# Sliding-window attention with a token-mixing MLP: q in one load per batch, queries reordered inside blocks, transposes on halves of the array, merged products, relus and copies, a new hand-written order

## The chip, the core and the metric

The kernel runs on one core of one Trainium2 chip. The metric is device time in microseconds of one execution, lower is better. A profile is one execution recorded by the hardware; its span runs from the first to the last instruction of the core.

The engines that matter: PE (TensorE; its weight loads are shown as PEld), DVE (VectorE), ACT (ScalarE), POOL (GpSimd, which here issues casting loads), and SP (SyncE, which issues stores).

## The reference, cut to what matters

q, k and v are 8 batches x 8 heads x 576 tokens x 64. Attention sees the last 128 tokens, with a linear distance bias per head; the heads' outputs are laid side by side as x (576 x 512 per batch), and x is mixed over tokens.

```python
scores = q @ k^T / 8                                     # per batch and head
scores = where(0 <= i - j < 128, scores - slope_h * |i - j|, -1e9)
attn   = softmax(scores)
x      = (attn @ v) with heads side by side              # (8, 576, 512)
wq, wk = x @ moe_w_q, x @ moe_w_k                        # (8, 576, 64)
mixed  = (wq @ wk^T / 8) @ x                             # = wq @ (wk^T @ x) / 8
out    = relu(mixed) @ moe_w_out                         # (8, 576, 512), f32
```

## The kernel before

Everything on chip is f16 except PSUM and the output. A batch's tokens are cut into four blocks of 128 and a tail of 64; tails of two batches (a pair, `pr`) are handled together, and so is the MLP of a pair. One operation (`Op`) is a short list of instructions for one engine; the whole sequence of operations is written out by hand in `ORDER`, one word per operation: its name, its batch and part, then the engine (P, A, D, G or S) and, for TensorE, which of the 4 PSUM pairs (of 2 banks each) or which single bank it writes. Each engine runs its operations in the order of that text, and semaphores join engines where data or banks are shared. So a change of `ORDER` moves every engine's queue.

The operations, by name:

- Loads. `LF`: the first tiles of batch 0 in f32 through SP and ACT. `Lq`, `Lk`, `Lv`, `Lt` (tails of q and k of a pair, two transfers): on GpSimd, with a cast to f16 on the way. Each moves 128 tokens of 8 heads, as 1024 pieces of 64 elements. `Lw`, `Lwo`: the MLP's weights in f32 through SP into output buffers (`osb`), cast by DVE in `CWQ` and `CW`.
- `TQ` (L474, transposes of q and k of one block by a product with the identity, 8 of 128x128, into one bank), copied out by `ETQ`; `TF`, `TJ` the same for batch 0, `TT`/`ETT` for tails, on the lower 64 rows of the array.
- `QK` (unit of key block g, four heads u): scores transposed, keys on partitions. Two heads share the array: one on rows 0 to 63, one on rows 64 to 127, writing two banks. `EXP` (L587) on ACT evicts 1024 columns; `MUL` (L594) on DVE multiplies them by a table `bias` of exp(-slope distance), zero outside the window (`biasl` for the last key blocks).
- `PV`: context of a block of queries; the 65th column of v is 1, so the sum of the weights comes along. `RC` takes the reciprocal, `X` (L634) evicts x. For the 64 tail queries all eight heads go into 64 partitions.
- `XT`/`EXT` and `XTT`/`EXTT`: transposes of x and their copies. `WQ`, `WK`, `WT`: projections of x, of a pair, and of its tails. `G`: wk^T x. `MX`: G with wq into mixed, transposed; two batches use the two row halves. `RM`, `RMT` (L770, L772): relu, 512 columns each. `OUT`: by moe_w_out, four products of 512 columns; `EO` evicts it into `osb`, `DO` stores it through SP.
- `WM`: products on zeros that keep TensorE busy at the start.

`wk`'s tail is kept with zeros in the other batch's rows (`pads`), since both tails lie in one tile. `NNAT` = 4, `NV` = 4 and `NPT` = 5 say how many buffers q and k tiles, v tiles and score tiles have; `OSB` = 12 output buffers.

The parts that decide the mode in which the array is used are the slices of the operands:

```python
mm(ps[:, e, ...], t[64 * e:64 * e + 64, 1, hp, ...], t[64 * e:64 * e + 64, 0, hp, ...])   # QK: row halves
mm(pw[64 * e:64 * e + 64, :], wqk_sb[:, c, 0:64], xT_s[b % NX][:, c, :])                  # WQ: column halves
tp(dst[:, j, c, :], src[j][:, 2 * c:2 * c + 2, :], identh)                                # TQ: whole array
```

Of the kernel before, what the change touches and what calls it, by code (L numbers as in the profile page):

```python
# [25 lines left out]
NNAT = 4  # L26
NV = 4
NPT = 5
PTW = 1088
# [4 lines left out]
OSB = 12  # L34
WIDE = ()

WARM = (12, 3, 4, 3, 3, 5,)

ORDER = """
warm:D LF0.0.1.0:A ident:G LF0.0.1.1:A LF0.1.0.1:S ones:D LF0.1.0.0:S Lk0.1:G LF0.0.0.1:S  # L40
LF0.0.0.0:S Lq0.2:G pads:D zeros:D Lt0:G WM.0:P31 TF0.1.1:P00 idh:D TF0.1.0:P01 iota:G Lk0.2:G
wmc:D WM.1:P31 TF0.0.1:P10 EF0.1.0:D EF0.1.1:D mask:G TF0.0.0:P01 EF0.0.1:A Lq0.3:G bias:A
EF0.0.0:D Lk0.3:G WM.2:P31 TJ0.2.0:P00 TJ0.1.1:P01 EJ0.2.0:D QK0.0.1:P1 Lq1.1:G EJ0.1.1:D
QK0.1.1:P0 QK0.0.0:P2 Lv0.0:G EXP0.1.1:A biasl:D TT0:P30 Lq1.2:G TJ0.2.1:P31 EXP0.0.0:A
QK0.1.0:P0 Lk1.1:G EJ0.2.1:D EXP0.0.1:A ETT0:D TJ0.3.0:P31 Lk1.2:G EXP0.1.0:A EJ0.3.0:D ETT1:D
WM.3:P21 TJ0.3.1:P10 Lv0.1:G QK0.2.1:P2 EJ0.3.1:D QK0.2.0:P3 MUL0.1.0:D QK0.3.1:P1 EXP0.2.0:A
Lk1.0:G QK0.3.0:P0 MUL0.0.0:D Lq1.0:G EXP0.2.1:A MUL0.2.0:D MUL0.0.1:D Lk1.3:G EXP0.3.1:A
MUL0.2.1:D PV0.0:P2 Lq1.3:G TQ1.1:P30 EXP0.3.0:A RC0.0:D MUL0.1.1:D TQ1.2:P31 Lv0.2:G ETQ1.1:D
ETQ1.2:A MUL0.3.1:D PV0.1:P0 Lv0.3:G X0.0:D QK1.1.0:P3 Lk2.1:G QK1.1.1:P1 RC0.1:D MUL0.3.0:D
EXP1.1.0:A TQ1.0:P20 Lq2.1:G X0.1:D EXP1.1.1:A ETQ1.0:D XT0.0:P21 Lv1.0:G QK1.0.0:P0 EXT0.0:D  # L50
Lq2.2:G TQ1.3:P20 EXP1.0.0:A MUL1.1.1:D QK1.0.1:P1 PV0.2:P3 Lk2.2:G ETQ1.3:D EXP1.0.1:A
MUL1.0.0:D QK1.2.1:P2 Lv1.1:G QK1.3.1:P0 RC0.2:D EXP1.2.1:A PV0.3:P1 X0.2:D Lq2.3:G RC0.3:D
QK1.2.0:P3 X0.3:D QK1.3.0:P2 Lk2.3:G EXP1.3.0:A MUL1.0.1:D TQ2.1:P10 Lv1.2:G MUL1.1.0:D
EXP1.3.1:A PV1.0:P2 MUL1.2.1:D XT0.1:P11 Lv1.3:G RC1.0:D MUL1.3.0:D EXT0.1:A Lv0.4:G TQ2.2:P00
ETQ2.1:D Lq2.0:G ETQ2.2:A X1.0:D WM.4:P01 PV1.1:P1 MUL1.3.1:D Lv1.4:G EXP1.2.0:A QK2.1.0:P0
QK2.1.1:P2 wz:D RC1.1:D Lw:S Lk2.0:G X1.1:D EXP2.1.0:A TQ2.3:P30 MUL1.2.0:D Lk3.1:G Lwo.1:S
XT1.0:P31 EXP2.1.1:A Lwo.3:S ETQ2.3:D PV1.2:P0 Lt1:G Lwo.2:S PV1.3:P1 EXT1.0:A RC1.2:D Lwo.0:S
X1.2:D PV0.4:P2 RC1.3:D RC0.4:D QK2.2.0:P0 X1.3:D Lq3.1:G EXP2.2.0:A X0.4:D Lk3.0:G WM.5:P30
PV1.4:P1 XT1.1:P31 RC1.4:D X1.4:D QK2.2.1:P0 Lq3.0:G EXT1.1:A XTT0:P30 CWQ:D Lv2.0:G TQ2.0:P10
EXP2.2.1:A EXTT0:D WK0:P31 ETQ2.0:D Lq3.2:G MUL2.1.1:D QK2.0.1:P1 EWK0:A Lk3.2:G QK2.0.0:P0  # L60
MUL2.2.0:D WT0:P30 EXP2.0.1:A WQ0:P31 Lv2.1:G EWT0:D EXP2.0.0:A MUL2.0.1:D G0:P30 CW.1:D EWQ0:A
CW.2:D TT2:P00 MUL2.0.0:D EG0:A Lv2.4:G ETT2:D MX0.4:P3 MX0.1:P1 ETT3:D MX0.0:P2 RMT0:A RM0.1:D
MX0.2:P0 RM1.0:A Lk3.3:G MX0.3:P3 RM0.2:D TQ3.1:P10 RM0.0:A RM0.3:D RM1.2:A Lq3.3:G QK2.3.1:P2
RM1.1:A CW.0:D QK2.3.0:P0 CW.3:D TQ3.0:P30 EXP2.3.1:A Lv2.2:G ETQ3.1:D OUT0.3:P11 ETQ3.0:D
Lk4.2:G EXP2.3.0:A PV2.0:P2 MUL2.1.0:D OUT0.1:P10 Lv3.1:G RM1.3:A RC2.0:D MUL2.3.0:D EO0.3:A
QK3.0.0:P3 Lv2.3:G QK3.0.1:P0 X2.0:D EXP3.0.0:A OUT1.0:P11 MUL2.3.1:D Lv3.0:G EO0.1:A TQ3.2:P20
MUL3.0.0:D OUT0.2:P21 EXP3.0.1:A Lk4.1:G ETQ3.2:D PV2.1:P3 Lq4.2:G EO1.0:A MUL3.0.1:D EO0.2:A
QK3.1.0:P0 QK3.1.1:P1 RC2.1:D Lq4.1:G MUL2.2.1:D EXP3.1.0:A TQ3.3:P20 X2.1:D OUT0.0:P21 Lv3.2:G
EXP3.1.1:A ETQ3.3:D PV2.2:P3 Lq4.0:G MUL3.1.0:D EO0.0:A QK3.2.1:P0 QK3.2.0:P1 RC2.2:D
EXP3.2.1:A Lq4.3:G OUT1.3:P21 X2.2:D MUL3.1.1:D Lv3.3:G EXP3.2.0:A PV2.3:P3 MUL3.2.1:D PV3.0:P0  # L70
OUT1.4:P20 Lk4.3:G EO1.3:A RC2.3:D RC3.0:D X2.3:D Lk4.0:G QK3.3.1:P1 X3.0:D EO1.4:A QK3.3.0:P3
XT2.0:P21 EXP3.3.0:A MUL3.2.0:D Lv3.4:G PV3.1:P0 EXT2.0:D TQ4.2:P20 Lt2:G EXP3.3.1:A MUL3.3.0:D
TQ4.1:P30 XT2.1:P21 RC3.1:D ETQ4.2:A MUL3.3.1:D OUT1.1:P31 Lv4.1:G ETQ4.1:D PV3.2:P1 EXT2.1:D
EO1.1:A Lk5.0:G OUT1.2:P30 RC3.2:D X3.1:D Lv4.0:G PV3.3:P2 X3.2:D EO1.2:A QK4.1.1:P0 Lv4.2:G
RC3.3:D TQ4.3:P30 X3.3:D EXP4.1.1:A QK4.1.0:P1 Lk5.1:G ETQ4.3:D PV2.4:P2 EXP4.1.0:A XT3.0:P31
RC2.4:D TQ4.0:P30 Lq5.0:G X2.4:D EXT3.0:A PV3.4:P0 ETQ4.0:D QK4.2.0:P2 Lq5.1:G XT3.1:P10
RC3.4:D EXP4.2.0:A X3.4:D QK4.2.1:P3 Lq5.3:G TT4:P11 EXT3.1:D EXP4.2.1:A QK4.0.1:P0 Lk5.3:G
XTT2:P20 MUL4.1.1:D WK2:P10 EXP4.0.1:A EXTT2:D Lk5.2:G ETT5:D WT2:P20 ETT4:D EWK2:A Lq5.2:G
MUL4.2.0:D QK4.0.0:P0 QK4.3.1:P3 EWT2:A QK4.3.0:P1 MUL4.2.1:D EXP4.0.0:A WQ2:P21 Lq6.3:G
MUL4.1.0:D EXP4.3.1:A G2:P20 Lv4.3:G MUL4.0.1:D MUL4.0.0:D EWQ2:A Lk6.0:G PV4.2:P3 MUL4.3.1:D  # L80
# [77 lines left out]
def kernel(  # L158
# [53 lines left out]
    def natv(b, j, n):  # L212
        return nat_s[(b // 2) % 2][j][n][:, b % 2]
# [13 lines left out]
    def hold(i):  # L227
        held.append(i.ins)
# [686 lines left out]
```

## Time and profile before

| | us |
|---|---|
| three runs: median (lowest, highest) | 141.13 (140.97, 143.18) |
| the profiled execution | 141.15 |
| its span | 139.3 |
| TensorE clock granted, mean over the span | 0.987 |
| mean of one MUL (128x1024) on DVE, 64 of them | 0.68, 0.67 |
| mean of one EXP (128x1024) on ACT, 64 of them | 1.03 |
| mean of one RM (128x512) on ACT, 25 of them; on DVE, 7 | 0.65; 0.68 |
| mean of one output eviction on ACT, 35 of them; on DVE, 1 | 0.60; 0.69 |
| mean of one x eviction, 128x512, 32 of them; of the tails, 64x512, 8 | 0.69; 0.69 |
| transfers of q, k, v, tails on GpSimd | 30, 31, 40, 8 |
| landing of a q tile, a k tile, a v tile, half a pair's tails (medians) | 5.1, 5.3, 5.5, 7 to 8 |

How to read it: matmuls are pipelined and their ends are modelled, so a duration of a matmul holds some 0.2 us in which the next has begun; from start to start they are much shorter. On DVE and ACT neighbours overlap by about 0.1. The slices are 40 equal parts of the span, each digit the busy share in tenths.

### The profile page before, as it was taken

To read this page: it belongs to the slowest core of one execution; us is meant where nothing else is said; L and a number is where in the kernel's file an instruction comes from. 1 tells how busy PE (TensorE), PEld (TensorE's weight loads), DVE (VectorE), ACT (ScalarE), POOL (GpSimd) and SP (SyncE) were. 2 spreads that over 40 slices of the span, in tenths; PEclk is the share of its full clock that TensorE was granted. 3 is DMA by queue.
4 is the path that set the end of the run, shared out by engine and by line. 5 is a ranking of instruction groups with operands and counts; after the bars stand their busy time and mean duration, and the time that the engine had idled before them with its cause. 6 is when DMAs were issued, how large, how long until landed. Compare 5 with 4: busy or idle time off the path is not lost.

```text
span 139.3 us, 4479 instructions
## 1 busy us (share of the span) xinstructions
PE 125.9 (90%) x1846; PEld 84.5 (61%) x1846; DVE 114.1 (82%) x254; ACT 112.2 (81%) x165; POOL 95.6 (69%) x118
## 2 busy tenths in 40 slices
PE   6778599879987999999999999999999999999970
PEld 4445486768744566767866477667765656754420
DVE  5657999999996999999999999999998999705000
ACT  3089969898796999868999999978989995279860
POOL 7999999999919999999999999759940000000000
PEclk9999869999999999999999999999999999999999
DMA  4999999999999999999999999999999975505993
GB/s 103 184 155 154 157 153 153 152 150 177 283 184 156 152 155 152 151 153 150 152 151 154 147 172 270 232 202 152 157 171 272 338 274 216 226 5 171 335 355 121
DMA packets 119332, 25.59 MB, mean 184 GB/s; under 512 B 114192, under 2 KB 114192, under 8 KB 119312
## 3 DMA queue, kind: packets, MB, share of 16 engines
q0 software_dynamic: 109264, 13.77, 155.9%
q1 hardware_dynamic: 8992, 11.28, 24.2%
q10 hardware_dynamic: 1056, 0.26, 0.8%
q8 instruction: 14, 0.23, 0.6%
q14 instruction: 6, 0.05, 0.1%
HBM read 29.62 MB, written 9.44 MB: 280 GB/s over the span
## 4 chain that ended last, share of the span: by engine, by line
PE 58%; POOL 22%; DMA 7%; DVE 7%; issue 2%; ACT 1%; ACTq 0%; POOLq 0%
PE pair L231 47%; POOL nat L363 13%; PE pair L234 11%; DMA natt<-in_k_dram 7%; POOL vt L380 6%; DVE pt L594 3%; DVE qkT L240 2%; POOL natt L370 2%; ACT osb L238 1%; DVE x L634 1%; DVE xT L240 0%; DVE rm L772 0%; POOL wm L298 0%; DVE xTt L240 0%; POOL wm L300 0%
## 5 line engine op out<-in xcount | busy, mean ns | idle before, releaser
L587 ACT ACTIVATE pt<-pair 128x1024 f16<-128x1024 f32 x64 | 62.8, 1033 | 4.0 <-PE pair L231 3.6
L380 POOL DMA_DIRECT2D vt<-in_v_dram x40 | 36.9, 976 | 2.6 <-PE pair L231 2.4
L363 POOL DMA_DIRECT2D nat<-in_k_dram x31 | 30.8, 1036 | 3.5 <-DMA nat<-in_k_dram 3.4
L231 PE MATMUL pair<-wout_sb,rm 128*128 128x512 f16 x128 | 31.6, 379 | 0.0
L594 DVE TENSOR_TENSOR pt<-pt,bias 128x1024 f16<-128x1024 f16 x48 | 31.3, 680 | 0.1
L363 POOL DMA_DIRECT2D nat<-in_q_dram x30 | 30.4, 1039 | 0.3 <-DMA vt<-in_v_dram 0.3
L238 ACT COPY osb<-pair 128x512 f32<-128x512 f32 x35 | 20.7, 601 | 7.4 <-PE pair L231 7.2
L231 PEld LDWEIGHTS <-pt 128*128 128x128 f16 x576 | 21.4, 98 | 8.4 <-issue 2.7
L231 PE MATMUL pair<-vt,pt 128*128 128x65 f16 x576 | 24.1, 195 | 2.3 <-ACT pt L587 1.6
L240 DVE COPY qkT<-pair 128x1024 f16<-128x1024 f16 (+1 forms) x38 | 21.7, 591 | 2.6 <-PE pair L231 1.3
L231 PE MATMUL pair<-qkT 64*128 64x256 f16 (+2 forms) x320 | 21.5, 250 | 1.1 <-DVE x L634 0.5
L634 DVE TENSOR_TENSOR x<-pair,inv 128x512 f16<-128x512 f32 x32 | 21.6, 685 | 0.5
L234 PE MATMUL pair<-identh,nat 128*128 128x128 f16 x244 | 19.3, 226 | 1.4 <-ACT pt L587 0.7
L234 PEld LDWEIGHTS <-nat 128*128 128x128 f16 x244 | 15.2, 101 | 5.8 <-issue 3.6
L231 PEld LDWEIGHTS <-rm 128*128 128x128 f16 x128 | 11.1, 97 | 10.6 <-issue 0.8
L231 PEld LDWEIGHTS <-qkT 64*128 64x128 f16 x320 | 11.3, 94 | 7.7 <-issue 3.2
L770 ACT ACTIVATE rm<-pair 128x512 f16<-128x512 f32 x25 | 13.7, 647 | 0.0
L594 DVE TENSOR_TENSOR pt<-pt,biasl 128x1024 f16<-128x1024 f16 x16 | 10.7, 668 | 0.0
L234 PE MATMUL pair<-identh,x 128*128 128x128 f16 x128 | 9.9, 219 | 0.0
L648 DVE RECIPROCAL inv<-pair 128x8 f32<-128x8 f32 (+1 forms) x40 | 7.8, 200 | 1.2 <-PE pair L231 0.8
L234 PEld LDWEIGHTS <-x 128*128 128x128 f16 x128 | 7.6, 98 | 1.7 <-issue 0.8
L240 DVE COPY xT<-pair 128x1024 f16<-128x1024 f16 x12 | 8.2, 687 | 0.4 <-PE pair L234 0.2
(66 smaller groups left out, 116.7 us busy)
## 6 DMA issues: line engine op xcount, KB each, us to landing
out_dram<-osb SPq DMA_DIRECT2D x32, 256.0 KB, 3.0
vt<-in_v_dram POOLq DMA_DIRECT2D x32, 128.0 KB, 5.5
nat<-in_k_dram POOLq DMA_DIRECT2D x31, 128.0 KB, 5.3
nat<-in_q_dram POOLq DMA_DIRECT2D x30, 128.0 KB, 5.1
osb<-in_moe_w_out_dram SPq DMA_DIRECT2D x4, 256.0 KB, 7.2
out_dram<-osb SPq DMA_DIRECT2D x8, 128.0 KB, 3.9
osb<-in_q_dram SPq DMA_DIRECT2D x4, 128.0 KB, 3.8
natt<-in_q_dram POOLq DMA_DIRECT2D x4, 128.0 KB, 7.1
```

The lines of the kernel that those rows point to most:

```text
L231: hold(nc.tensor.matmul(*a, **k))
L234: hold(nc.tensor.transpose(*a))
L238: hold(nc.scalar.copy(out_ap, in_ap))
L240: hold(nc.vector.tensor_copy(out=out_ap, in_=in_ap))
L363: return lambda: nc.gpsimd.dma_start(out=natv(b, j, n), in_=(q, k)[j][b, :, P * n:P * n + P, :].transpose([1, 0, 2]))
L370: nc.gpsimd.dma_start(out=natt_s[pr % 2][:, j].rearrange("p e h d -> p (e h) d"), in_=(q, k)[j][2 * pr:2 * pr + 2, :, 512:576, :].rearrang ...
L380: return lambda: nc.gpsimd.dma_start(out=vtv(b, t)[:n, :, 0:D], in_=v[b, :, P * t:P * t + n, :].transpose([1, 0, 2]))
L587: nc.scalar.activation(out=pt[:, 0:1024], in_=two(s.bank).rearrange("p e c -> p (e c)"), func=AF.Exp, scale=SCALE)
L594: ENG2[o.eng].tensor_tensor(out=pt[:, 0:1024], in0=pt[:, 0:1024], in1=bt, op=ALU.mult)
L634: nc.vector.tensor_tensor(out=x[r].rearrange("p (g h d) -> p g h d", g=2, h=4), in0=sums(p)[r, :, :, 0:64], in1=box["inv"][r].unsqueeze(3) ...
L648: nc.vector.reciprocal(out=box["inv"][r], in_=sums(p)[r, :, :, 64])
L770: hold(nc.scalar.activation(out=out_ap, in_=in_ap, func=AF.Relu, scale=WSCALE))
```

## The change

What it does:

- q of a batch comes in one transfer (`Lq`, 128 partitions of 4 consecutive tokens, so pieces of 256 elements) instead of four. Column r of partition p is token 4p + r; after the transpose a block holds its queries in the order (r, x) for token 4x + r. The mask and the table follow that order, and `RM` stores the relu back in token order, elements 4 apart.
- `TQ` is now q of a whole batch, 32 transposes of 128x64, alternating between the two column halves of the array, into two banks with pieces of 32 elements; one copy `ETQ` of 2048 columns (1024 before). k is `TK`: two blocks at once, transposes split into two row halves (`tp2`), two banks, one copy `ETK`.
- `XT`, `XTT`, `TT` and batch 0's `TJ` are split into row halves by `tp2` too; q tails now lie on partitions 0 to 63 and k tails on 64 to 127.
- One `MUL` of 2048 columns for two `EXP`; one table for all blocks (three parts of 128 columns per head, 384 in all), so `biasl` is gone. `NPT` = 6.
- The tail queries' `PV` put heads 0 to 3 on output partitions 0 to 63 and heads 4 to 7 on 64 to 127, in one bank; x tails are 128x256; `XTT`, `WT` and the last part of `G` follow.
- `RM` evicts both banks at once, 1024 columns.
- The MLP's weights are loaded by GpSimd with a cast on the way, four transfers; `Lw`, `Lwo` on SP and the casts `CWQ`, `CW` are gone.
- `OUT` of the last block of batch 7 is cut into two halves of 256 columns. `OSB` = 14. `NNAT` = 3 for k, two buffers for q.
- `ORDER` is new throughout. The warm-up products are 19, 2, 4 and 7 instead of 12, 3, 4, 3, 3 and 5. `LOGB` is empty, so the paths that ask for it are not used.

```diff
-NNAT = 4
+NNAT = 3
+NQ = 2
+QR = 4
-NPT = 5
+NPT = 6
-OSB = 12
-WARM = (12, 3, 4, 3, 3, 5,)
+OSB = 14
+GROUPS = ((0, 1), (2, 3), (4, 5), (6, 7))
+LAST = (7, 3)
+WARM = (19, 2, 4, 7,)
...
+    def tp2(o, m, lo, hi):
+        for r, x in enumerate((lo, hi)):
+            k = slice(64 * r, 64 * r + 64)
+            tp(twoh(o.bank)[:, r, 64 * m:64 * m + 64], x[k], identh[k, k])
...
+    def dma_q(b, r0):
+        return lambda: nc.gpsimd.dma_start(
+            out=natq_s[b % NQ][r0 // QR:P].rearrange("p h r d -> p h (r d)"),
+            in_=q[b, :, r0:512, :].rearrange("h (p r) d -> p h (r d)", r=QR))
...
-            wto = []
-            for c in range(4):
-                lwo = add("Lwo", "", c, next(i), {"SP": (0.9, 5.0)}, [wz], lambda o, c=c: nc.sync.dma_start(
-                    out=wide32(c), in_=moe_w_out[P * c:P * c + P, :]))
-                wto.append(add("CW", "", c, -1.0 + 0.1 * c, EV(0.59, 0.4), [lwo],
-                               lambda o, c=c: cp(o.eng, wout_sb[:, c, :], wide32(c))))
+            wto = [load(("Lwo", c, ""), next(i), [lambda c=c: nc.gpsimd.dma_start(
+                out=wout_sb[:, 2 * c:2 * c + 2, :],
+                in_=moe_w_out[256 * c:256 * c + 256, :].rearrange("(c p) n -> p c n", p=P))], 1, [])
+                for c in range(2)]
...
-            for j in range(2):
-                for c in range(NHP):
-                    tp(
-                        dst[:, j, c, :],
-                        src[j][:, 2 * c:2 * c + 2, :].rearrange("p a b -> p (a b)"), identh)
+                for c in range(NHP):
+                    for r in range(QR):
+                        for e in range(2):
+                            dst = twoh(o.bank)[64 * e:64 * e + 64, c // 2].rearrange(
+                                "p (c t r x) -> p c r t x", c=2, t=4, r=QR)[:, c % 2, r]
+                            tp(dst, natq_s[b % NQ][:, 2 * c + e, r, :], identh)
...
+            def emk(o):
+                for i in range(2):
+                    for c in range(NHP):
+                        x = natk(b, n + i)[:, 2 * c:2 * c + 2, :].rearrange("p a b -> p (a b)")
+                        tp2(o, 2 * c + i, x, x)
...
-            ENG2[o.eng].tensor_tensor(out=pt[:, 0:1024], in0=pt[:, 0:1024], in1=bt, op=ALU.mult)
-        mul[b, g, u] = add("MUL", b, f"{g}.{u}", w + 1.6, DVE(0.68),
-                           [x, mkb if g < 3 else mkbl], ml)
+            nc.vector.tensor_tensor(out=pv, in0=pv, in1=bt, op=ALU.mult)
+        mul[b, g, 0] = mul[b, g, 1] = add("MUL", b, g, w + 1.6, DVE(1.21), [xs[b, g], x, mkb], ml)
...
+            if qt == 4:
+                px = one(o.bank)
+                for h in range(4):
+                    for i, kb in enumerate((3, 4)):
+                        for g in range(2):
+                            mm(px[64 * g:64 * g + 64, 65 * h:65 * h + 65], ptc(kb, 4 * g + h, kb == 4, 64),
+                               vtv(b, kb)[:, 4 * g + h, 0:65], start=(i == 0), stop=(i == 1))
...
-                    tp(dst[:, c, n, :], x_s[b % NX][2 * i + n][:, P * c:P * c + P], identh)
+                    x = x_s[b % NX][2 * i + n][:, P * c:P * c + P]
+                    tp2(o, 2 * c + n, x, x)
...
-                    relu(o.eng, rm_s[pr % 2][:, db, e, :], two(t.bank)[:, e, :])
+                relu(o.eng, rm_s[pr % 2][:, db].rearrange("p e (t x r) -> p (e t) r x", t=4, r=QR),
+                     two(t.bank).rearrange("p e (t r x) -> p (e t) r x", t=4, r=QR))
...
+            def ev(o, t=t, box=box):
+                box["o"] = spool.tile([P, DM], FP32, name="osb", tag="osb", bufs=OSB)
+                cp(o.eng, box["o"][:, 0:256], one(t.bank)[:, 0:256])
```

The end of the order, from the last pair's tail transposes on, before:

```
XTT6:P10 WK6:P11 EXTT6:D WT6:P10 EWK6:A WQ6:P20 EWT6:A G6:P10 EWQ6:A EO4.2:A OUT5.4:P20 EG6:A DO4.2:S
MX6.4:P1 MX6.2:P0 EO5.4:A MX6.3:P3 RMT6:D RM7.2:A DO5.4:S MX6.0:P2 MX6.1:P1 RM7.3:A DO4.3:S OUT7.4:P01
...
```

and after:

```
XTT6:P2 OUT5.4:P00 EXT7.1:D EO2.0:D EXTT6:A WK6:P30 DO2.0:S DO3.3:S WT6:P01 EWK6:A WQ6:P31 EWT6:A
EO5.4:A G6:P01 EWQ6:A OUT5.2:P00 EG6:A MX6.4:P3 MX6.1:P2 EO5.2:D MX6.0:P1 RM6.1:A OUT5.3:P01 RMT6:D
...
```

## The prediction

> **What bounds the kernel now.** I read the page's first two parts, then busy time by stage, the chain, single stretches of TensorE's timeline, and the groups by shape.
>
> ```profile
> PE 125.9 (90%) x1846; PEld 84.5 (61%) x1846; DVE 114.1 (82%) x254; ACT 112.2 (81%) x165; POOL 95.6 (69%) x118
> ...
> PE   6778599879987999999999999999999999999970
> DVE  5657999999996999999999999999998999705000
> ACT  3089969898796999868999999978989995279860
> ```
>
> ```profile
> 0.00:42.40 42.40, 33.95 (x496) 25.16 (x496) 35.91 (x100) 31.66 (x40) 38.19 (x52) 0.96 2.03 167
> 42.40:121.20 78.80, 78.28 (x1234) 52.84 (x1235) 75.82 (x150) 69.39 (x102) 57.38 (x67) 1.00 1.99 190
> 121.20:139.30 18.10, 13.69 (x121) 6.45 (x118) 2.40 (x4) 11.16 (x23) 0.00 (x0) 0.99 0.55 195
> ```
>
> Columns of the second: stage, length, then busy TensorE, weight loads, DVE, ACT, POOL. Three stages: a start fed by loads; a middle with TensorE at 99% and DVE at 96%; and from WK6 at 121.2 a tail, the last pair's MLP. TensorE's 99% holds its pipeline's overlap, so below I go by starts. ACT has room: 88% in the middle.
>
> ```profile
> 14.04 3.51 POOL nat L363 x4
> ...
> 32.57 9.87 DMA natt<-in_k_dram
> ```
>
> The chain: GpSimd issues loads without a pause, one per 3.51/4 = 0.87 us, and the start ends when the second pair's tail load, issued from 31.8, has landed at 42.4.
>
> ```profile
> 53.80 0.61 PE L231 MATMUL pair<-qkT 64*128 64x256 f16 x8
> 54.34 1.04 PE L231 MATMUL pair<-wout_sb,rm 128*128 128x512 f16 x4
> ...
> 62.54 0.39 PE L231 MATMUL pair<-qkT 64*128 64x256 f16 x4
> 62.86 0.62 PE L234 MATMUL pair<-identh,nat 128*128 128x128 f16 x8
> 63.41 0.39 PE L231 MATMUL pair<-qkT 64*128 64x256 f16 x4
> ...
> 83.55 0.28 PE L231 MATMUL pair<-wqT,gs 64*128 64x64 f16 x8
> 83.76 0.62 PE L234 MATMUL pair<-identh,nat 128*128 128x128 f16 x8
> ...
> 122.31 0.32 PE L231 MATMUL pair<-xTt,wqk_sb 128*64 128x64 f16 x8
> 122.46 0.82 PE L231 MATMUL pair<-xT,wqk_sb 128*64 128x512 f16 x6
> ```
>
> Start to start, eight half-array score products take 0.54 us and four take 0.32, so a pair on the two row halves costs 0.11 and the change of mode behind it 0.10. Full transposes: 0.55 for eight, less 0.10 for the change, is 0.057 each. Four row-half pairs of 64 columns take 0.21, less 0.10: 0.029 a pair. Four column-half pairs take 0.15: 0.038 a pair.
>
> ```profile
> L594 DVE TENSOR_TENSOR pt<-pt,bias 128x1024 f16<-128x1024 f16 x48 | 31.3, 680 | 0.1
> L240 DVE COPY qkT<-pair 128x512 f16<-128x512 f16 x13 | 5.1, 418 | 2.1 <-PE pair L231 1.3 <-PE pair L234 0.6
> ```
>
> The same copy takes 681 ns at 1024 elements, so 512 f16 elements cost 0.26 us. Neighbours on DVE overlap by 0.08 (two x evictions take 1.29 where one is 0.685): 1024 occupy 0.60, 2048 should occupy 1.13.
>
> **TensorE, part by part.** Transposes by row halves: k, 124 x 0.057 = 7.1 becomes 124 pairs x 0.029 = 3.6; x with its tails, 144 x 0.057 = 8.2 becomes 4.2; tails of q and k, 64 on one row half at about 0.029 = 1.9, become 32 pairs, 0.9. Together -8.5. q goes by column halves of 128 columns: 112 pairs at 0.057 and 16 short pairs, 6.9 against 120 x 0.057 = 6.8: nothing. Context products of the last 64 queries, by column halves: 128 x 0.029 = 3.7 becomes 64 x 0.038 = 2.4: -1.3. The tail projection grows from 16 products and 16 pairs (1.1) to 48 pairs (1.6): +0.5; two more warm-ups, +0.2. Sum -9.1. Counted in the two instruction orders, TensorE changes between whole array, row halves and column halves 96 times before and 119 after: 23 x 0.095 = +2.2. Net -6.9.
>
> Two rules of the Trainium skill speak against this. "TensorEngine Tiling (Array Packing)", Tiling Modes, says that changing the mode drains TensorE; the trace agrees, with 0.10 us a change; without that rule the net would be -9.1. "TensorE: Matmul & The Clock Gate", LDWEIGHTS, gives columns/1.2 ns for a weight load and the tiling page's Restrictions say that column tiling loses the fast one; by these I estimate 53 ns for each of the 256 q loads, 13.7 us if none overlap, and a net of -0.1. The 0.038 of a column-half pair, with two weight loads in it, disagrees.
>
> **DVE.** Products: 64 x 0.60 = 38.4 becomes 32 x 1.13 = 36.2, -2.2. Tail x evictions are 128x256 instead of 64x512: 8 x 0.27 = -2.2. q and k copies -0.8 (q's save an overhead each, one tail copy goes to ACT); xT and xTt copies moved to ACT -1.6; three relus of 1024 for seven of 512, -0.8; casts of weights gone, 4 x 0.34 + 0.43 = -1.8; the second bias table gone -1.8; memsets -0.9. Against these eight more output evictions, two of them halves, +4.3; G and tail-projection copies +1.1. Sum -6.7. The tail gets 2.4 more of what is left (evictions, relus), so up to WK6 it is -9.1.
>
> **ACT.** Exponentials unchanged. Output evictions 35 to 28, -3.8; relus nil (25 at 0.48 start to start, 13 at about 0.91, an exponential's pace at that size); the wider bias table +0.9; q, k, xT and xTt copies +3.1; others -0.5. Sum -0.3; up to WK6 about +0.9.
>
> The merged relu stores its f16 eight bytes apart, which no row does: between nothing and double, +11 us on ACT. I take nothing, since copies into 128-element pieces ran at the pace of plain ones, and keep the double for a rival.
>
> **Loads.** 109 transfers become 91: q 30 to 8, weights' four come to GpSimd. By 0.87 each the stream ends some 17 us sooner, and no compute waits there. The second tail load now stands behind 32 others, four short: near 29, landing near 39 with the same 9.9. A q load now holds four tiles; its landing lies between 5.1 (q now) and 7.2 (256 KB of w_out), and each batch's transpose stands over 8 us behind it: hidden; uncovered it would cost 2 us in one batch. Weights cast in flight leave SP's queue to q's first tiles and the outputs; nothing there waits on them.
>
> **New waits.** A product waits for both exponentials; on DVE, reciprocals and x evictions queue behind it, and the context products wait for it: 0 to 0.9 us a time, covered while another unit's work stands ahead, as the order mostly has it. Transposes take two of eight banks instead of one: about four bank holds more per batch on some 33.
>
> **The sum.** DVE up to WK6: 121.2 - 9.1 = 112.1. TensorE sheds as much there: 6.9, and 1.9 because twelve output products (4 x 0.22) stand behind WK6 instead of ten. ACT's work before WK6 is 31.66 + 69.39 + 0.9 = 102; with 8 idle in the start (10.7 before, of 42.4) and 95% from 39 on, T = 102 + 8 + 0.05 (T - 39) gives 113.7. I add 0.9 for the last pair's transposes, where ACT waits: WK6 at 114.6. The tail, 18.1 before, has 1.9 more products, less 0.8 of holes that they now fill and 0.25 for a half-size last eviction: 18.9. Span 133.5. The profiled execution took 141.15 with a span of 139.3, so 1.85 lie around it, and the median is 141.13: both bases agree. 135.3, taken as 135.0.
>
> **Rivals.** (a) ACT binds at the middle's pace: 39 + (102 - 31)/0.90 = 117.9, so 138.6. For: 88% is all it reached. Against: most of its waits were for TensorE. Chance 0.09.
> (b) The q transposes write four runs of 32 elements, a shape no row has; at double, 7 us more TensorE: 121.2 - 9 + 7 = 119.2, so 140.0. "PSUM — Partial Sum Buffer", Specifications, says non-contiguous patterns slow matmuls significantly, which would be this case; no run here shows it. The runs are whole, so 0.07, with waits for banks of that size.
> (c) Slower: two half-array transposes don't run side by side. Products do in the trace; no two transposes on different halves are in it. At 0.029 or 0.057 each: k 7.2, x 8.4, tails 1.9, q 13.8, against 15.6 counted above: +15.7, at the engine that is 99% full before WK6: 121.2 + 6.7 = 127.9, so 148.6. It decides once a 64-column pair costs over 0.05 us. Chance 0.05.
> (d) The relus' stores at half rate: +9 on ACT before WK6, T = 123, so 145. Chance 0.04. Rest 0.01.
>
> **How the numbers follow.** The forecast has 0.74, its own range 131 to 138.3: the low end is the DVE bound (112.1 + 18.9 + 1.85 = 132.9) with 2 us of the start's holes closed too. Over all cases 130.5 to 141.5; outside lie (c), (d) and little else. A measurement of this kernel tells about 2% from no change (138.3, 144.0). Faster 0.72 + 0.04 + 0.03 = 0.79; same 0.11; slower 0.10.
>
> **What would show it.** Eight natk transposes in about 0.12 us and a change of mode; 32 natq in about 0.9; products at 1.21, merged relus at 1.03 on ACT, tail x evictions near 0.42; WK6 near 114.6 with ACT above 90% in the middle; the second tail load landing near 39. I am wrong if pairs take 0.05 or more, if relus take over 1.3, or if TensorE shows holes behind exponentials.

## The result, and the profile after

The changed kernel is slower. Four runs have a median of 156.9 us (156.26 to 159.47); the four runs of the kernel before beside them have 141.24 (140.97 to 143.18). The ratio is 1.11, with an interval of 1.102 to 1.118. Ratios, here and below, leave out runs more than 1.5% above the fastest of their kernel; medians and ranges hold all runs. The profiled execution took 157.46 with a span of 155.7, against 141.15 and 139.3. Forecast were 135.0 and a range up to 141.5.

The page of the kernel after, its busy times and its slices:

```profile
PE 126.5 (81%) x2312; PEld 80.8 (52%) x2312; DVE 113.7 (73%) x194; ACT 129.0 (83%) x146; POOL 79.4 (51%) x103
...
PE   7887688998855999999898479799964998986790
...
DVE  4656999999778579889998346879995788356211
ACT  0398999997899997899998999789899975779660
...
PEclk9968999999999999999999758999999999999999
```

DVE's work fell only from 114.1 to 113.7, and ACT's rose from 112.2 to 129.0. ACT is at 7 to 9 in nearly all of the middle. TensorE and DVE, at 9 almost throughout before, now have dips (3 to 6) at nearly the same places, and one of them lies at two intervals of half TensorE clock (87.8 to 94.6 us).

Busy time by stage, with the columns of before (stage, length, TensorE, weight loads, DVE, ACT, POOL, clock, DMA share, GB/s); the cuts are the second pair's landed tails and the start of WK6:

```profile
0.00:38.70 38.70, 31.42 (x629) 22.60 (x630) 31.53 (x67) 30.03 (x36) 36.00 (x53) 0.96 1.97 164
38.70:133.20 94.50, 78.89 (x1543) 50.47 (x1540) 75.21 (x120) 85.25 (x93) 43.40 (x52) 0.96 1.42 153
133.20:155.70 22.50, 16.14 (x145) 7.70 (x143) 6.94 (x9) 13.76 (x18) 0.00 (x0) 1.00 0.53 188
```

The start is shorter (38.7 against 42.4), with the second pair's tails landing near 39 as forecast. The middle grew from 78.8 to 94.5 and the tail from 18.1 to 22.5; ACT has 90% of the middle, TensorE 83% (99% before).

The groups by shape, where the cause stands in one number (mean ns of one behind the busy time):

```profile
L638 ACT ACTIVATE pt<-pair 128x1024 f16<-128x1024 f32 x64 | 62.2, 1044 | 3.4 <-PE pair L234 3.2
L859 ACT ACTIVATE rm<-pair 128x1024 f16<-128x1024 f32 x13 | 30.6, 2498 | 0.8 <-PE pair L234 0.8
...
L653 DVE TENSOR_TENSOR pt<-pt,bias 128x2048 f16<-128x2048 f16 x32 | 38.6, 1216 | 1.5 <-ACT pt L638 1.4
...
L861 DVE TENSOR_SCALAR rm<-pair 128x1024 f16<-128x1024 f32 x3 | 7.3, 2433 | 2.1 <-PE pair L234 2.0
```

An exponential evicts 1024 f32 columns from PSUM in 1.04 us; the merged relu (L859), of the same size on the same engine, takes 2.50, and on DVE 2.43. Before, two relus of half the size took 2 x 0.65. What this does to TensorE is in its timeline (start, duration, idle time before in brackets):

```profile
43.02 0.39 PE L234 MATMUL pair<-wqT,gs 64*128 64x512 f16 x2
44.18 0.39 PE L234 MATMUL pair<-wqT,gs 64*128 64x512 f16 x2 [0.77 <-ACT rm L859]
```

Each mixed product (MX) fills a PSUM pair that a relu must empty; TensorE comes to the next use of the pair and waits about a microsecond. The list of waits (us in total, times, longest) sums them up:

```profile
PE pair L234 <- ACT rm L859: 10.4, 10, 1.6
```

The chain of waits puts 13% of the span on the relu.

Two questions are left: is the relu's store the whole loss, and, since the prediction had expected a gain of 6, where is that gain once the store is mended?

### The profile page after: what moved, and what is told of

Its sections match the earlier page's. It is cut to its first block, busy times and chain, and to the rows that moved or that the text cites. A ratio compares the mean times of both kernels' runs of the same rounds, so it can differ in the third digit from the quotient of the medians.

```text
span 155.7 us, 5327 instructions
## 1 busy us (share of the span) xinstructions
PE 126.5 (81%) x2312; PEld 80.8 (52%) x2312; DVE 113.7 (73%) x194; ACT 129.0 (83%) x146; POOL 79.4 (51%) x103
## 4 chain that ended last, share of the span: by engine, by line
PE 47%; ACT 24%; issue 11%; DVE 11%; DMA 4%; POOL 1%; DVEq 0%; ACTq 0%; POOLq 0%
PE pair L234 41%; ACT rm L859 13%; ACT pt L638 7%; PE pair L237 6%; DMA natk<-in_k_dram 4%; DVE pt L653 3%; DVE qkT L248 2%; DVE x L714 2%; ACT osb L246 2%; ACT qkT L246 2%; DVE xtl L708 1%; ACT xT L246 1%; DVE inv L704 1%; DVE xT L248 1%; POOL natq L379 0%
## 5 line engine op out<-in xcount | busy, mean ns | idle before, releaser
L653 DVE TENSOR_TENSOR pt<-pt,bias 128x2048 f16<-128x2048 f16 x32 | 38.6, 1216 | 1.5 <-ACT pt L638 1.4
L234 PE MATMUL pair<-wout_sb,rm 128*128 128x512 f16 (+1 forms) x132 | 32.4, 377 | 2.0 <-DVE rm L861 0.8
L859 ACT ACTIVATE rm<-pair 128x1024 f16<-128x1024 f32 x13 | 30.6, 2498 | 0.8 <-PE pair L234 0.8
L375 POOL DMA_DIRECT2D natk<-in_k_dram x31 | 27.7, 915 | 1.5 <-DMA natq<-in_q_dram 1.2
L234 PE MATMUL pair<-vt,pt 128*128 128x65 f16 (+1 forms) x576 | 22.3, 195 | 4.9 <-ACT rm L859 2.5
L234 PEld LDWEIGHTS <-pt 128*128 128x128 f16 (+1 forms) x576 | 19.1, 101 | 11.0 <-issue 6.7
L248 DVE COPY qkT<-pair 128x1024 f16<-128x1024 f16 (+2 forms) x29 | 19.8, 703 | 6.0 <-PE pair L237 2.7
L237 PE MATMUL pair<-identh,natq 128*64 128x128 f16 (+1 forms) x256 | 9.2, 229 | 2.2 <-ACT pt L638 0.8
L237 PEld LDWEIGHTS <-natq 128*64 128x64 f16 (+1 forms) x256 | 8.2, 117 | 3.7 <-issue 1.4
L861 DVE TENSOR_SCALAR rm<-pair 128x1024 f16<-128x1024 f32 x3 | 7.3, 2433 | 2.1 <-PE pair L234 2.0
```

Of the source, the lines that this page charges most:

```text
L234: hold(nc.tensor.matmul(*a, **k))
L237: hold(nc.tensor.transpose(*a))
L248: hold(nc.vector.tensor_copy(out=out_ap, in_=in_ap))
L375: return lambda: nc.gpsimd.dma_start(out=natk(b, n), in_=k[b, :, P * n:P * n + P, :].transpose([1, 0, 2]))
L653: nc.vector.tensor_tensor(out=pv, in0=pv, in1=bt, op=ALU.mult)
L859: hold(nc.scalar.activation(out=out_ap, in_=in_ap, func=AF.Relu, scale=WSCALE))
```

## Experiments on the relu

**e1_store_order.** The relu stores plainly, and the output transfer puts the tokens back in order.

```diff
-relu(o.eng, rm[:, db].rearrange("p e (t x r) -> p (e t) r x", ...), two(t.bank).rearrange("p e (t r x) -> p (e t) r x", ...))
+relu(o.eng, rm[:, db].rearrange("p e t -> p (e t)"), two(t.bank).rearrange("p e t -> p (e t)"))
-nc.sync.dma_start(out=out[b, P * st:P * st + P, :], in_=osb)
+nc.sync.dma_start(out=out[b, P * st:P * st + P, :].rearrange("(x r) n -> r x n", r=QR), in_=osb)
```

> The changed kernel, but the relu stores plainly, in the order it reads, and the output transfer puts the rows back in token order (same 2 KB rows). Theory S (the f16 store 8 bytes apart is what costs): merged relus at 1.03 us on ACT and 1.13 to 1.22 on DVE instead of 2.50 and 2.43; 13 x 1.47 = 19 us off ACT and 3.7 off DVE; time 135 to 139, near the prediction's sum. Rival P (a merged relu is slow because it reads two banks that TensorE works beside): relus stay at 2.4 to 2.5, time 155 to 158. Rival B (the store is only a part, waits for banks and mode changes cost the rest): relus at 1.03, but time 141 or more.

It took 186.29 us (185.26 to 187.86), ratio 1.3205 [1.3078, 1.3331]. The relus fell to 1026 ns, as expected, but the end of the kernel is now its stores: the chain puts 23% of the span on them, and in most of the last twelve slices of 40 the core moves 102 GB/s, where the kernel after moves up to 381 in its last twelve. The outermost dimension of the store is 4 instead of 128. The Trainium skill, "DMA: Bandwidth & Descriptors", Why a DMA increments its semaphore by 16 and not by 1, says that the number of engines used is the largest up to 16 that divides the slowest dimension of both sides; that would be 4 here, and the drop agrees. The run prices the relu, but says nothing of the total: rival B's "141 or more" is met, but by the stores, not by waits for banks.

**e2_read_order.** The permutation goes to the other side of the same instruction: PSUM is read 128 bytes apart, SBUF is written in order. The two access patterns alone:

```diff
-out "p e (t x r) -> p (e t) r x", in "p e (t r x) -> p (e t) r x"
+out "p e (t x r) -> p (e t) x r", in "p e (t r x) -> p (e t) x r"
```

> The changed kernel, but the relu does the reordering on its reading side: it reads PSUM at steps of 128 bytes and stores contiguous f16. Theory S: relus at 1.03 (ACT) and 1.13 to 1.22 (DVE), time as with the plain store, 135 to 139. Rival: any stepped side costs, then relus at about 2.5 and time about 157.

Ten runs have a median of 141.55 (140.49 to 143.52), ratio 0.9991 [0.9945, 1.0037]. Groups by shape:

```profile
L859 ACT ACTIVATE rm<-pair 128x1024 f16<-128x1024 f32 x13 | 12.6, 1026 | 0.8 <-PE pair L234 0.8
L861 DVE TENSOR_SCALAR rm<-pair 128x1024 f16<-128x1024 f32 x3 | 3.7, 1225 | 0.1
```

The strided read costs nothing: 1026 ns on ACT and 1225 on DVE are what e1 has with plain access on both sides. One instruction's access pattern takes back 15.4 us. What remains is a kernel as fast as the one before, 141.55 and not the 135 to 139 that theory S expected.

**e3_before_stepped.** The kernel before, with nothing changed but the relu's store, 8 bytes apart; tokens are left in that order, so the output's rows differ.

```diff
-relu(o.eng, rm_s[pr % 2][:, db, e, :], two(t.bank)[:, e, :])
+relu(o.eng, rm_s[pr % 2][:, db, e, :].rearrange("p (t x r) -> p t r x", t=4, r=4),
+     two(t.bank)[:, e, :].rearrange("p (t r x) -> p t r x", t=4, r=4))
```

> The kernel before, with only its 512-column relus' store made to step 8 bytes (columns of a block permuted, so the output's rows come in another order inside blocks). Theory S: 0.18 + 512 x 2.26 ns = 1.34 us on ACT for 0.65 and about 1.29 on DVE for 0.68; 25 x 0.69 + 7 x 0.61 = 21 us of engine time, time 150 to 158. Rival P: relus stay at 0.65 to 0.70, time 141.

One run: 156.67, span 154.9. Groups by shape:

```profile
L770 ACT ACTIVATE rm<-pair 128x512 f16<-128x512 f32 x25 | 30.4, 1393 | 0.0
...
L772 DVE TENSOR_SCALAR rm<-pair 128x512 f16<-128x512 f32 x7 | 8.6, 1308 | 1.6 <-PE pair L231 1.6
```

In the kernel before, the same groups are:

```profile
L770 ACT ACTIVATE rm<-pair 128x512 f16<-128x512 f32 x25 | 13.7, 647 | 0.0
...
L772 DVE TENSOR_SCALAR rm<-pair 128x512 f16<-128x512 f32 x7 | 4.5, 677 | 0.5 <-PE pair L231 0.5
```

The one line makes the old kernel as slow as the new one, inside theory S's range.

**e4_steps.** To price the store, e1 with the four relus of a batch stored in steps of 4, 8, 16 and 32 bytes (each line its own step); here too the rows stay where the step puts them.

```diff
+R = (2, 4, 8, 16)[db]
+dst = rm_s[pr % 2][:, db].rearrange("p e (t x r) -> p (e t) r x", t=4, r=R)
+src = two(t.bank).rearrange("p e (t r x) -> p (e t) r x", t=4, r=R)
```

> As the plain-store kernel, but the four relus of a pair store f16 at steps of 4, 8, 16 and 32 bytes (output rows in another order inside blocks). One look for the price by step. If what costs is how many elements fall into one 16-byte line: 4 bytes (four a line) at 1.03, 8 bytes (two a line) at 2.5, 16 and 32 bytes (one a line) at 2.5 or more. If any step other than one costs the same: all four at 2.5. If the price comes from short rows of the pattern (64, 32, 16, 8 elements), it rises from each to the next.

The whole took 206.39 (one run). Groups by shape, L897 for 4 bytes, L899 for 8, L901 for 16, L903 for 32:

```profile
L897 ACT ACTIVATE rm<-pair 128x1024 f16<-128x1024 f32 x4 | 5.5, 1363 | 0.0
L899 ACT ACTIVATE rm<-pair 128x1024 f16<-128x1024 f32 x3 | 7.9, 2627 | 0.8 <-PE pair L234 0.8
L901 ACT ACTIVATE rm<-pair 128x1024 f16<-128x1024 f32 x2 | 9.4, 4707 | 0.0
L903 ACT ACTIVATE rm<-pair 128x1024 f16<-128x1024 f32 x4 | 18.4, 4590 | 0.0
```

The time about doubles with the step up to 16 bytes and then stands; DVE's relus do the same (2453 ns at 8 bytes, 4750 at 16). This fits a price for each visit to a 16-byte line: 1024 elements make 256, 512, 1024 and 1024 visits, and the times are about 0.2 us and 4.4 ns a visit (1.33, 2.45, 4.7, 4.7). The step of 4 bytes, expected at the plain 1.03, already costs. The Trainium skill, "SBUF — State Buffer", Specifications (TRN2), says lines are 16 bytes and asks for two hits a line for full bandwidth. The line's size agrees; the two hits do not, for a store: 8-byte steps have them and take 2.4 times as long.

## Experiments on the gain that did not come

e2 holds the rest of the change. By its trace the work did shrink: from 45 us to WK6, counted from start to start, TensorE's work is 9.4 us less than before. But in the same stretch its holes of over 0.3 us grew by 5.6, changes of mode by 1.3 and small gaps by 1.1, and WK6 came at 119.8, not at the forecast 114.6.

**e5_act_added, e6_dve_added, e7_pe_added; b5_before_act, b6_before_dve, b7_before_pe.** Work is added to one engine, beside the second exponential or the product of each step, or by issuing the first two of a step's four score products twice, in e2 and in the kernel before.

```diff
+            if u == 1: nc.scalar.copy(spare, warm[:, 0:160])        # e5, b5: 32 x 0.215 us
+            nc.vector.reciprocal(out=spare, in_=ones8)              # e6, b6: 32 x 0.112 us
-            for a in range(2):                                      # e7, b7
+            for a in (0, 0, 1):
```

> The kernel with relus that store whole pieces (141.55 us, span 139.0, WK6 at 119.8), and behind every second exponential one more copy of 128x160 on ACT, which nothing reads: 32 copies at about 0.2 us start to start (0.83 ns an element from the exponentials, and the 0.07 us that a small copy adds), 6.4 us of added ACT work, all of it before WK6. Theory A (ACT sets the pace of the middle, my rival (a)): nearly all of it appears, 141.5 + 5 to 6.5 = 146.5 to 148. Theory D (as forecast, DVE and TensorE set it and ACT has room): at most +2, so 141.5 to 143.5. Theory L (no engine binds; the written orders make all three wait for each other in turn, and work costs what its engine's share of the chain of waits says, ACT 5%): +0.3, so 142.

> The same kernel, and behind each of the 32 merged products one more reciprocal of 128x8 on DVE, which nothing reads: 32 x 0.19 = 6.1 us of added DVE work before WK6. Theory A: DVE has 12 us of idle before WK6, so at most +2: 141.5 to 143.5. Theory D: nearly all of it, 146.5 to 147.5. Theory L (DVE 27% of the chain): +1.6, so 143.

> The same kernel, with the first four score products of each of the 64 score steps issued twice (the second overwrites the first): 64 x 0.22 = 14 us less what the last block's smaller pieces save, about 13 us of added TensorE work before WK6. Theory A: TensorE has holes, but 13 us is more than they are: +5, so 146. Theory D: nearly all, 152 to 155. Theory L (TensorE 54% of the chain): +7, so 148.5.

> The kernel before (141.2 us), with the same 32 ACT copies of 128x160 behind every second exponential as in the run on the changed kernel, where they took 0.215 us start to start, 6.9 us in all, and cost 3.9 us of time. Theory P (the kernel before was packed against DVE and TensorE, as I read it, and ACT had room): at most +2, so 141 to 143. Theory L (the written orders couple all three engines in both kernels): about as in the changed kernel, +3 to 4.5, so 144 to 145.5.

> The kernel before with the 32 reciprocals of 128x8 on DVE, one behind every second bias product, which took 0.112 us start to start behind a product (3.6 us in all) and cost 3.7 us in the changed kernel. Theory P: all of it, +3.6 to 6, so 145 to 147. Theory L: +2 to 4.

> The kernel before with two of the products of each score step issued twice (160 more products, 80 pairs on the two row halves: 64 score steps, 48 pairs of 256 columns at 0.108, 16 of 192 and 16 of 64: 7 us; in the changed kernel they cost 5.7 us; what I put down there as 14 us counted each pair twice). Theory P: TensorE is 99% full in the middle, so nearly all of it, +6 to 7: 147 to 148. Theory L: +4 to 6, 145 to 147.

(The expectation of e7 counted each pair twice; the edit adds 160 products, 80 pairs, 7 us. That of e6 counted whole durations; from start to start the reciprocals add 3.6 us, not 6.1.)

| added, us | to before | to e2 |
|---|---|---|
| ACT, 6.9 | 145.08, 1.0253 [1.0192, 1.0314] | 145.07, 1.027 [1.018, 1.036] |
| DVE, 3.6 | 144.67, 1.0209 [1.0137, 1.0281] | 144.93, 1.0278 [1.0217, 1.0338] |
| TensorE, 7.0 | 145.69, 1.0304 [1.0228, 1.0381] | 146.94, 1.041 [1.0343, 1.0477] |

No engine takes added work for nothing, and none binds alone: of what is added to ACT about half arrives at the end, of TensorE's 0.6 to 0.8, of DVE's nearly all, in both kernels (by the ratios to before 3.6 and 3.9, 4.3 and 5.9, 3.0 and 4.1 us, each known to about 1 us). On e2 each result lies between the ranges of its theories; on the kernel before, theory L's ranges hold all three. (The traces of e5 and e6 hold one more interval at half clock, so their shares may be too high.) A microsecond saved on TensorE or ACT was thus not worth a whole one, and ACT, which I had read as 88% busy with room, passes on half.

**e8_half_loads.** e2 with half the heads of k and v loaded for batches 4 to 7.

```diff
-out=natk(b, n), in_=k[b, :, P * n:P * n + P, :].transpose([1, 0, 2])
+out=natk(b, n)[:, 0:hh(b)], in_=k[b, 0:hh(b), P * n:P * n + P, :].transpose([1, 0, 2])      # and v alike
```

> The same kernel, where k and v of batches 4 to 7 are loaded for four of the eight heads alone (the other heads keep what the buffers held, so those outputs differ): some 36 of 40 transfers at half the bytes and half the rows. Theories A, D and L: loads are not what the middle waits for beyond single waits of under 1 us, so 140 to 141.5. Rival Q (the stream of loads, slowed by the 512 KB q loads that GpSimd stands behind, holds the middle back): the 2.5 us that TensorE loses at 80 to 90 us come back, and some of the waits before, 137 to 139.

141.1, ratio 0.9995 [0.9958, 1.0031], as theories A, D and L expected. Lighter k and v alone brought nothing. q still came in full, and in the trace the next experiment's wait stood as in e2 (3.3 us).

**e9_no_false_wait.** That wait is in e2's list of DVE's waits, and in one stretch of its timeline:

```profile
DVE invt L701 <- PE pair L234: 3.3, 4, 0.9
```

```profile
53.10 0.18 DVE L701 RECIPROCAL invt<-pair 128x4 f32<-128x4 f32 x1 [0.86 <-PE pair L234]
53.32 0.42 DVE L708 TENSOR_TENSOR xtl<-pair,invt 128x256 f16<-128x256 f32 x1
53.66 1.22 DVE L653 TENSOR_TENSOR pt<-pt,bias 128x2048 f16<-128x2048 f16 x1
```

The reciprocal of a tail's sums reads one bank of a PSUM pair; TensorE meanwhile writes an output block's four products into the other. The kernel tells the framework which steps use separate halves, but the tail's reciprocal and its x eviction, which the change made single-bank, are not in that list, so the reciprocal waits for the four foreign products, with the next bias product queued behind it. The edit enters them:

```diff
+        if op.kind == "RC" and op.part == 4:
+            src = op.deps[0]
-                nc.vector.reciprocal(out=box["inv"], in_=sums(p)[:, :, 64])
+                hold(nc.vector.reciprocal(out=box["inv"], in_=sums(p)[:, :, 64]))     # and X of the tail alike
```

> The kernel with relus that store whole pieces (141.55 us, WK6 at 119.8), and the reciprocals and scalings of the last 64 queries (RC and X, part 4) entered in the same lists of independent PSUM halves as every other single-bank step. Nothing is computed differently. In the kernel as it stands four of these eight reciprocals start 0.85 to 0.95 us after everything that they read is there: they wait for the four output products that TensorE makes into the other half of the same pair of banks, DVE stands behind them, and ACT's output evictions of that half (up to 1.1 us late) and the next products wait for the scaling in turn. Theory W (this wait is where the forecast gain went): 4 x 0.9 = 3.6 us of DVE's idle time before WK6 go, WK6 near 116.5, 137.5 to 139. Rival C (the three engines are coupled by the order anyway, and a wait that goes comes back as another): within 1 us of 141.5. Rival L (loads set the rest): the same, since transfers stay as they are.

140.46 (138.61 to 141.07), ratio 0.984 [0.9779, 0.99]: 1.1 us by the medians, 2.1 by the ratios. The wait is gone but for one case:

```profile
DVE invt L703 <- PE pair L234: 0.5, 1, 0.5
```

The profiled execution (141.04, near the top of the range) holds an interval at half TensorE clock, so its WK6 (120.0) does not tell where the gain lies; theory W's 116.5 is not shown.

**e10_new_order, e13_order_margin.** Twice a new order of e9's operations on all engines, GpSimd's loads included, chosen by replaying the operations with traced durations (e10 with those of a trace taken before e9's); e13 with a margin for loads.

```diff
-TensorE: QK1.1.1 QK1.0.1 QK1.1.0 TJ0.3.1 QK1.0.0 TK1.1 QK0.3.1 QK0.3.0 ...
+e10:     QK1.0.1 QK1.0.0 WM.2 TJ0.3.1 TK1.1 QK1.1.1 PV0.0 QK1.1.0 ...
```

> The same kernel as the one without the wait on the other half, with its written order changed: some operations a few places earlier or later, other banks and in places the other of ACT and DVE for an eviction, chosen by replaying the operations with the durations of the trace of the kernel with plain relu stores. Work, loads and instructions are the same in kind. Replayed in that way the order takes 2.1 us less than the one it replaces. Theory W with an order that still holds slack: 2 us under the run without the wait, 135.5 to 137. Rival C: the replay knows only what it was given, and the gain does not appear, within 1 us of that run.

> The kernel without the wait on the other half with its written order changed on all engines, chosen by replaying the operations with traced durations, where now each load counts as landing 2 us later than traced and the outputs share the transfers' time (the order tried before let loads be needed as they landed, and stalled at 58 to 68 us). Replayed it takes 1.5 us less than the order it replaces. Theory Q: 138 to 139.5. Rival C: the replayed gain does not appear, 140 us or more.

144.56, ratio 1.0224 [1.0181, 1.0267], and 145.63, ratio 1.0306 [1.0271, 1.0341]: neither replayed gain appeared. e10 is slower than both of its theories have it, e13 lies in rival C's open range. In e10 the q of batch 4 landed 10.9 us after its issue, against 7.6 in e2 and 7.4 in e9, and TensorE stood for it:

```profile
60.29 1.08 PE L237 MATMUL pair<-identh,natq 128*64 128x128 f16 x32 [2.16 <-DMA natq<-in_q_dram]
```

e13 showed what no replay held, a stop inside one operation:

```profile
74.42 0.39 PE L234 MATMUL pair<-wout_sb,rm 128*128 128x512 f16 x1
76.57 0.81 PE L234 MATMUL pair<-wout_sb,rm 128*128 128x512 f16 x3 [1.76 <-issue]
```

One of four products is issued, nothing that the profile shows is waited for, and the second comes 2.15 us later. Such stops occur in e2, e9, e12 and others too, at some of the places where TensorE's count of instructions (weight loads and products) stands, within one, at 187 above a multiple of 256. From start to start e2 has three of 0.5 to 0.7 us, e9 three of 0.4 to 1.1, e12 four of 0.4 to 1.7, e13 five of 0.5 to 2.1; the kernel before, e8, e11 and e14 have none over 0.35. In e2 and e12 one such place is behind the ninth of sixteen transposes of the same step; e12:

```profile
89.57 0.31 PE L237 MATMUL pair<-identh,natk 64*128 64x64 f16 x9
91.39 0.29 PE L237 MATMUL pair<-identh,natk 64*128 64x64 f16 x7 [1.51 <-issue]
```

The page has a queue that carries instructions (packets, MB, share), 14 transfers of 16 KB before and 18 in the kernel after:

```profile
q8 instruction: 14, 0.23, 0.6%
```

```profile
q8 instruction: 18, 0.29, 0.7%
```

The kernel before has 3692 instructions on TensorE, the changed one 4624, since a transpose on two halves is two loads and two products. That is 264 and 257 instructions for each transfer, and 259 in e14 (4144 over 16), so one transfer may well bring 256. In the traces most stops end 2.3 to 2.7 us after such a transfer starts. From 45 to 92 us, with the loads running, it starts 2.5 to 4.5 us after the last boundary in e2, e9 and e12, and under 2.3 in e11 but for once. Together that is 5 to 7 us, and these three kernels use 256 instructions up in 5.8 to 7.6 us there, where before takes 6.3 to 9.4 from 51 us on.

**e11_half_loads_q and b8_before_half.** q, k and v of the later batches with half the heads, on e9 and on the kernel before.

```diff
-in_=q[b, :, r0:512, :]
+in_=q[b, 0:hh(b, 4), r0:512, :]        # and its tile, k and v alike
```

> The kernel without the wait on the other half (140.46 us, 138.6 to 141.1), where q, k and v of batches 4 to 7 are loaded for four of the eight heads alone (the other heads keep what the buffers held, so those outputs differ). In its trace most loads between 38 and 81 us land 0.2 to 2 us before their first use, q of the last batch is followed by a 1 us stall, and TensorE's clock is halved from 84.5 to 87.9 behind it. Theory Q (with the wait gone the transfers are what holds it): the stalls at 52 to 90 us go, 137.5 to 139. Rival C (the order couples the engines, and transfers hold nothing): 140 to 141.

> The kernel before (141.3 us), with q, k and v of batches 5 to 7 loaded for four of the eight heads alone (the other heads keep what the buffers held, so those outputs differ). Theory Q (only the changed kernel runs into its transfers): 140.5 to 141.5. If the kernel before was held by them too, 138 to 140.

e11 lightens batches 4 to 7, b8 batches 5 to 7. e11: 136.87 (136.16 to 137.24), ratio 0.9677 [0.9645, 0.9709], below theory Q's 137.5 to 139. b8: 141.42, 1.0006 [0.9961, 1.0051], as its theory Q has it. The middle stage, of e2 and then of e11:

```profile
38.50:119.80 81.30, 76.25 (x1544) 48.80 (x1539) 72.37 (x120) 71.56 (x93) 44.44 (x53) 1.00 1.65 178
```

```profile
38.50:116.10 77.60, 75.44 (x1548) 48.85 (x1548) 73.06 (x123) 71.49 (x94) 39.18 (x52) 1.00 1.20 145
```

The same work in 3.7 us less, e9's change included; the stops at 256 instructions are gone. So the new kernel is held by its transfers, by 2.3 us against e9 by the ratios (3.6 by the medians). The old one is not, as far as b8 goes: it reads the same 29.6 MB from HBM, of which b8 takes off 4.9 and e11 6.6.

**e12_loads_sorted.** e9 with nothing but GpSimd's list in another order, by first use.

```diff
-Lk1.3 Lk0.3 Lk1.2 Lv0.0 Lv0.2 Lv0.1 Lq2.0 Lv0.4 Lv0.3 Lk2.1 Lk2.0 ...
+Lk0.3 Lk1.3 Lk1.2 Lv0.0 Lv0.2 Lv0.1 Lk2.1 Lq2.0 Lv0.3 Lk2.0 Lv0.4 ...
```

> The same kernel as the one without the wait on the other half, all loads in full, with GpSimd's list alone in another order: transfers that are used soon stand ahead of those that stood in their buffers for 10 to 25 us (a k tile of batch 7 and v tiles of batches 4 to 7). Every other engine's list is as it was. Theory Q: q of batches 5 and 7 and k of batches 4 and 5 land 1 to 4 us sooner, their stalls go, 139 to 139.8. Rival C: no change, 140 to 141.

139.59 (138.34 to 141.42), ratio 0.9861 [0.9815, 0.9908]: the lowest median of a version that computes everything, 1.4% under the kernel before. From e9 (0.984) the intervals do not tell it apart, so a gain from sorting is not shown. In its profiled execution (141.42, the top of the range) stops at 256 instructions remain (up to 1.7 us).

**e14_whole_kx.** e12 with the transposes of k and x by whole tiles again: 480 instructions fewer, and by the prediction's prices 8 us more of TensorE's work (240 transposes at 0.057 for pairs at 0.029, and 14 changes of mode at 0.095).

```diff
-                        tp2(o, 2 * c + i, x, x)
+                        tp(whole(o, 2 * c + i), x, identh)        # and x alike, with the copies' patterns
```

> The kernel without the wait on the other half and with the transfers sorted (139.6 us), with two parts of the change undone: k and x are transposed by whole tiles of the array again, 240 instead of 480 transposes, into the first of the two banks that each step holds; order, evictions' sizes and everything else as they were. TensorE's instructions fall by 480 of 4624. By the terms of the forecast TensorE gets k 3.5 and x 4.0 us back and 14 more changes of mode, 1.3: 8.8 us, and added TensorE work cost 0.8 of itself before: 146 to 147. Theory F (the stalls of 0.5 to 2 us at every 256th of TensorE's instructions, which wait for a 16 KB instruction transfer behind the loads, eat what half-array pairs save, as there are twice as many of them): 139 to 142.

140.96 (140.81 to 141.53), ratio 0.9981 [0.9937, 1.0024], as theory F expected: 1.4 us more than e12 by the medians, 1.7 by the ratios, not 8. The page has 16 instruction transfers, and no stop at a boundary exceeds 0.2 us. TensorE is busy for 80.14 of 81.80 us from 38.5 to 120.3 us, in e2's middle for 76.25 of 81.30. The half-array transposes of k and x thus bring 1.4 to 1.7 us; the rest of their saving stood in waits.

## Why the prediction was wrong

**The sign: "I take nothing".** The step that failed is the relu's store. The prediction named it as the one access that no row shows, put its cost "between nothing and double, +11 us on ACT", and took nothing, because copies into 128-element pieces ran at full pace. That row was of the wrong kind: it cuts an access into long runs, while the store leaves gaps inside each line. Measured are 2.5 us against 1.03, +19 us on ACT for 13 relus and +3.6 on DVE for three. Rival (d) had this mechanism and decided the result, but its end of the range was also too near: factor 2.4 instead of 2, and 145 us instead of 156.9. Of these 11.9 us, 6.5 are the forecast that it starts from (below), and 5.4 the price of the store: 15.4 measured against 10. Its sum let ACT's time alone grow, while the trace shows TensorE waiting 10.4 us for PSUM pairs that a relu held. "Merged relus 1.03 on ACT, wrong if over 1.3" was the right thing to look for.

**The size: saved work was taken as saved time.** With the store mended, 135.0 stands against 141.55. The mis-sized term of the sum is ACT's "95% from 39 on". ACT's work before WK6 came as forecast (30.03 and 71.56 in e2, 101.6 for 102), but ACT stood 9.7 us of e2's middle, 88% busy as before, where the sum allows 3.7 and 0.9. That is about the 5.2 us by which WK6 comes late. Three steps lie behind it; the changes of e9 and e11 together take back 4.4 us by the ratios, and the rest stays unexplained.
- "Loads: the stream ends some 17 us sooner, and no compute waits there." GpSimd's last load is issued near 91 us in e2, near 102 before, so 11 us sooner and not 17, since GpSimd stands for q's large loads (below). q, k and v are the same bytes, and come denser: k and v tiles land 6.5 us after issue in e2 (5.3 and 5.5 before), q's loads 7.8 to 8.0, beyond the 7.2 I had as upper bound. With lighter loads and e9's change (e11) the kernel takes 136.87, near the forecast, and the old one gains nothing from a similar lightening (b8).
- The new waits that I listed left out the false one on the tail's half pair: 1.1 to 2.1 us (e9).
- The transposes' gain, counted per pair, ignored that each pair is four instructions; whether fetching them is the reason is argued, not shown. Of k's and x's saving of some 8 us e14 finds 1.4 to 1.7.

GpSimd's wait for q in e2 (us in total, times, longest):

```profile
POOL vt L393 <- DMA natq<-in_q_dram: 6.8, 5, 1.8
```

"ACT has room" fell as well, and so did "DVE up to WK6" as the only bound, though DVE passes on nearly all: added work arrives from all three engines in both kernels.

**What held.** The half-array prices, by the timeline of after:

```profile
60.93 1.08 PE L237 MATMUL pair<-identh,natq 128*64 128x128 f16 x32
61.95 0.41 PE L237 MATMUL pair<-identh,natk 64*128 64x64 f16 x16
62.29 1.04 PE L234 MATMUL pair<-wout_sb,rm 128*128 128x512 f16 x4
```

From start to start 32 q transposes take 1.02 us and 16 k transposes 0.34: less one change of mode at 0.095, 0.058 and 0.030 a pair (forecast 0.057 and 0.029). So rivals (b) and (c) fell: scattered PSUM writes and halves side by side cost nothing. Bias products took 1.216 us (1.21) and tail x evictions 0.420 (0.42). That the second tail load landed near 39 (38.5) was luck: it was issued at 32.7, not near 29, and landed 5.8 us later, not 9.9. The tail of e2 took 19.2 us (18.9); after has 22.5, with the last pair's four stepped relus in it. Rival (a), ACT alone binding at 138.6, fell too: e5 passes on half, not all. Its pace of 90% was nearer to e2's 88% than the sum's 95%.

**What stays open.** That the stops at 256 instructions are late instruction transfers is inferred from their place, the transfers' times and their absence in e11 and e14; no run moved instructions off the DMA engines. e11 lightens data and makes room for instructions at once, so its 2.3 us are not split between the two. Against the stops as the main cause speaks e8: its trace has none over 0.35 us, where e2's three add up to 1.8, and it is no faster than e2. Why e11 gains where e8 did not, the lighter q or the wait that e9 removed, is open too.

## What to carry to other kernels

Of an access that no row shows, count how many 16-byte lines a store touches, and put the permutation on the side that reads PSUM; take the bad end for the forecast when the cheap row is of another kind. A saved microsecond of one engine is worth a whole one only if adding a microsecond costs a whole one: that can be measured before a large change is made. Splitting instructions to save array time uses up the instruction stream faster, so look at its transfers when the loads are dense; here this is a suspicion, not a measured cause.

## What the hardware showed that I had not expected

- A stepped f16 store costs ACT and DVE alike some 4.4 ns for each visit to a 16-byte line (1.36, 2.6, 4.7 and 4.6 us for 1024 elements at 4, 8, 16 and 32 bytes on ACT; 2.45 and 4.75 at 8 and 16 on DVE), a PSUM read in 128-byte steps nothing (1.03).
- While the loads were dense, TensorE stood for up to 2.1 us from start to start at some of the boundaries of 256 instructions (five of 18 in e13).
- In e9 TensorE's clock halved for one interval without an idle interval ahead of it. Its windows there (length, then busy TensorE, weight loads, DVE, ACT, POOL, clock, DMA share, GB/s):

```profile
81.10:84.50 3.40, 2.24 (x45) 1.32 (x43) 3.33 (x7) 3.40 (x4) 2.93 (x4) 1.00 2.43 156
84.50:87.90 3.40, 3.40 (x43) 2.06 (x37) 1.53 (x3) 1.17 (x2) 3.38 (x5) 0.50 2.40 157
```

TensorE was busy for 2.24 of 3.40 us, with one stop of 1.1 us at an instruction boundary and smaller gaps, and ran the next 3.4 us at half clock. The Trainium skill, "TensorE: Matmul & The Clock Gate", What's actually happening, gives a free-running window of 3413 ns, which agrees with the length, and puts a whole idle window ahead of the half clock, which this does not show. The stop alone does not decide it: e12 has the same one without such an interval.
